# Second feed-forward product of 14 token blocks by Strassen's seven products, the first in pairs

## Chip, cores and metric

The kernel runs on one core of a Trainium2 chip. The metric is the device time of one execution in microseconds (us). TensorE (PE) multiplies, VectorE (DVE), ScalarE (ACT) and GpSimd (POOL) do the elementwise work, SyncE (SP) issues the DMAs.

## What is computed

Three stages on 8 x 576 tokens of 512 features, in fp32:

```python
scores = scale * np.matmul(q_c, k_c.transpose(0, 1, 2, 4, 3))      # attention inside chunks of 64 tokens, 8 heads
...
xn = (x - mu) / np.sqrt(var + 1e-06) * g_ln                        # feed-forward, 512 -> 2048 -> 512
ch = np.maximum(xn @ w_ch1, 0.0) @ w_ch2
return (x + ch).astype(np.float32)
...
h = x @ w_in                                                       # second stage: gated unit, mixing along the 576 tokens
h = 0.5 * h * (1.0 + np.tanh(c * (h + 0.044715 * h ** 3)))
v_s = np.einsum('ts,bsd->btd', w_sg, v_n) + b_sg[None, :, None]
return (x + gated @ w_out).astype(np.float32)
```

## The kernel before

The 4608 tokens are 36 tiles of 128, and two tiles make one of NB = 18 blocks of 256 tokens. Every fp32 product is made of three fp16 matmuls: each operand is split into a high and a low part, and high x high, high x low and low x high are added in PSUM.

**Attention** of a tile: QK (L273), maximum and difference (L308, L309), exp, sum (L314), reciprocal (L302), transposes (L283) through `pt`, PV (L292), and DVE's L322, which scales the result into the tile's x. All three PE steps of a tile use one PSUM pair (`pair1`), so the next tile's QK waits for L322. LayerNorm follows (L352, L353, L355), and `hl`, the split of it (ACT L358, POOL L360), goes by a transposing DMA into `xT`.

**Feed-forward** of a block b: `ff1(b, f)` for f = 0 to 15 multiplies 128 of the 2048 hidden features (12 matmuls of 256 columns into one bank, L511); ACT makes the high part (L515), DVE the low part (L516). `ff2(b, f)` uses them as stationary operand against 128 rows of w2 (6 matmuls of 512 columns, L532) and adds into two banks, one for each tile, over all 16 f. After the last, DVE adds the banks to x (two L544), SP stores x (L547, `x2d`), DVE takes its maximum (L184).

The order on each engine is made by a planner: each step is recorded with `op` (engine, assumed ns, reads, writes, priority), and `Plan.run` places them by these assumed times. In the FF blocks ff2 runs two f behind ff1, and the attention of later blocks is interleaved on PE. The first blocks go another way: the first products of blocks 0 and 1 are kept (`late`) until w2 is ready, and ff2 of blocks 1, 0 and 3 runs in rows of sixteen units without ff1 between.

While blocks 4 and on run, the **weights of the second stage** are prepared (`prep`: loads, L380 on DVE, L581 on ACT, a maximum through PE with `par`, a split with POOL L610), and the first x2 tiles are read back (`open_x2`, `first_x2`). After the last block the **second stage** follows: its first units are `v_unit` (L830); in it DVE's L818 and L916 and POOL's L856 and L906 are elementwise operations with two inputs in SBUF.

Of the kernel before, what the change touches and what calls it, by code (L numbers as in the profile page):

```python
# [127 lines left out]
def fused_kernel(ctx: ExitStack, tc, qkv, w1, w2, g1, w_in, w_out, wsgt, wsgs, g2, b_sg, out):  # L128
# [31 lines left out]
    mxc = small.tile([P, 5], F32, name="mxc")  # L160
# [76 lines left out]
    def palloc(tag, bufs, shape, dt, pool=None):  # L237
        return plan.buf(tag, bufs, lambda: (pool or pa).tile(shape, dt, tag=tag, name=tag, bufs=bufs))
# [215 lines left out]
    def scale_w2():  # L454
# [109 lines left out]
    def prep(nm, srcs):  # L564

        pr = 9000
        n = len(srcs)
# [500 lines left out]
```

## Time and profile before

| | |
|---|---|
| median of 3 runs | 1296.22 us (1293.89 to 1296.97) |
| profiled execution | 1294.67 us, span 1292.6 us |
| busy | PE 1246.9, DVE 672.2, ACT 477.2, POOL 260.2 us |
| mean granted clock of TensorE | 0.995 |

Attention of the first tiles and the preparation of w1 and w2 take the first part of the span, the FF blocks last until 877 us, the second stage takes the rest. "Idle before" or a bracket behind a row is the time in which the engine stood still ahead of that instruction, and behind the arrow what ended it. A matmul is listed with its latency; matmuls overlap, so the step from one start to the next is shorter. A clock of 1.00 is full speed.

### The profile page before, as it was taken

The page shows a single profiled execution, that of the slowest core. Times are in us where ns is not written, and L with a number is a line of the kernel's source. Part 1 is how long each engine was busy: PE and PEld are TensorE (multiplying, and loading weights), DVE is VectorE, ACT ScalarE, POOL GpSimd, SP SyncE. Part 2 cuts the span into 40 slices and gives each one's busy share as a digit, 9 for nine tenths or more (in the row PEclk, how much of TensorE's full clock was granted, in tenths as well). Part 3 has the DMA queues.
Part 4 walks back from the last instruction along what each step waited for, and adds up shares of the span by engine and source line. Part 5 has one row for each costly group of instructions (what it writes and reads, how often), then busy time and mean ns, then how long its engine had stood idle before and what let it go on. Part 6 is the DMA issues. An engine that isn't in the chain of part 4 may idle for free.

```text
span 1292.6 us, 23846 instructions
## 1 busy us (share of the span) xinstructions
PE 1246.9 (96%) x10111; PEld 774.2 (60%) x10111; DVE 672.2 (52%) x1381; ACT 477.2 (37%) x911; POOL 260.2 (20%) x291
## 2 busy tenths in 40 slices
PE   6899999999999999999999999999999998999998
PEld 4677645676666666666666666654544543554453
DVE  7895126434443244334324433217879479469564
ACT  5776302465321121122122112105745636537330
POOL 3342201042010010001001001003425035134120
PEclk9999999999999999999999999999999999999999
DMA  9963006522721131123113110002031240330101
GB/s 308 248 227 84 1 33 186 203 83 87 143 74 50 42 83 50 50 66 71 54 42 83 48 28 17 17 17 90 17 58 50 98 72 10 139 58 17 74 1 74
DMA packets 106378, 101.87 MB, mean 79 GB/s; under 512 B 79648, under 2 KB 79648, under 8 KB 106272
## 3 DMA queue, kind: packets, MB, share of 16 engines
q1 hardware_dynamic: 106272, 100.36, 27.9%
q8 instruction: 79, 1.29, 0.4%
q14 instruction: 27, 0.22, 0.1%
HBM read 62.59 MB, written 18.87 MB: 63 GB/s over the span
## 4 chain that ended last, share of the span: by engine, by line
PE 77%; DVE 12%; ACT 4%; DMA 3%; POOL 1%; issue 1%; SPq 1%; DVEq 0%; ACTq 0%; POOLq 0%
PE bank L511 25%; PE pair L532 23%; PE pb L892 8%; PE pb L874 7%; PE pb L954 4%; PE bank L532 3%; PE pb L830 2%; DVE gv L818 2%; DMA straw<-in_w 2%; DVE bs L838 1%; PE pair L273 1%; DVE gl L229 1%; DVE q L811 1%; PE pair L292 1%; ACT top L375 1%
## 5 line engine op out<-in xcount | busy, mean ns | idle before, releaser
L511 PE MATMUL bank<-xT,w1h 128*128 128x256 f16 x2304 | 393.0, 274 | 8.1 <-DVE hTl L516 3.7
L511 PE MATMUL bank<-xT,w1l 128*128 128x256 f16 x1152 | 315.1, 273 | 0.0
L516 DVE SCALAR_TENSOR_TENSOR hTl<-bank,hTh 128x256 f16<-128x256 f32 x256 | 108.0, 423 | 341.5 <-ACT hTh L515 340.1
L532 PE MATMUL pair<-w,hTh 128*128 128x512 f16 x896 | 266.5, 379 | 0.0
L511 PEld LDWEIGHTS <-w1h 128*128 128x128 f16 x2304 | 221.1, 98 | 70.7 <-issue 10.1
L515 ACT ACTIVATE hTh<-bank 128x256 f16<-128x256 f32 x256 | 97.7, 383 | 417.1 <-PE bank L511 416.9
L532 PE MATMUL pair<-w,hTl 128*128 128x512 f16 x448 | 169.8, 379 | 0.0
L532 PEld LDWEIGHTS <-hTh 128*128 128x128 f16 x1024 | 99.7, 98 | 75.1 <-issue 0.2
L511 PEld LDWEIGHTS <-w1l 128*128 128x128 f16 x1152 | 113.1, 98 | 13.5
L347 POOL TENSOR_SCALAR rs<-mv 128x1 f32<-128x1 f32 x36 | 8.6, 239 | 505.4 <-DVE mv L353 504.9
L830 PE MATMUL pb<-win,x2T 128*128 128x512 f16 x432 | 95.3, 379 | 0.9 <-DVE x L544 0.9
L874 PE MATMUL pb<-x2T,win 128*128 128x384 f16 x576 | 94.6, 326 | 0.0
L954 PE MATMUL pb<-wout,gh 128*128 128x512 f16 x288 | 85.7, 379 | 7.6 <-DVE x L959 7.6
L892 PE MATMUL pb<-wsg,vh 128*128 128x512 f16 x288 | 88.0, 380 | 0.0
L532 PEld LDWEIGHTS <-hTl 128*128 128x128 f16 x512 | 50.1, 98 | 60.4
L808 ACT ACTIVATE h<-pb,e2g 128x384 f32<-128x384 f32 (+1 forms) x84 | 52.0, 619 | 91.7 <-PE pb L874 57.9
L906 POOL TENSOR_TENSOR uT<-uT,vs 128x512 f32<-128x512 f32 x32 | 48.6, 1518 | 177.7 <-DVE vs L902 177.7
L874 PEld LDWEIGHTS <-win 128*128 128x128 f16 x576 | 56.2, 98 | 37.5
L811 DVE SCALAR_TENSOR_TENSOR q<-q,h 128x384 f32<-128x384 f32 (+1 forms) x84 | 52.0, 619 | 43.1 <-ACT q L809 43.1
L830 PEld LDWEIGHTS <-x2T 128*128 128x128 f16 x432 | 41.3, 98 | 50.4 <-issue 2.0
L360 POOL TENSOR_TENSOR hl<-xn,hl 128x512 f16<-128x512 f32 x36 | 44.5, 1237 | 70.2 <-ACT hl L358 70.0
L892 PE MATMUL pb<-wsg,vl 128*128 128x512 f16 x160 | 56.5, 380 | 0.0
(181 smaller groups left out, 1675.8 us busy)
## 6 DMA issues: line engine op xcount, KB each, us to landing
qk<-in_qkv SPq DMA_DIRECT2D x36, 512.0 KB, 3.9
straw<-in_w SPq DMA_DIRECT2D x16, 1023.8 KB, 6.4
v<-in_qkv SPq DMA_DIRECT2D x36, 256.0 KB, 3.2
x2d<-x SPq DMA_DIRECT2D x36, 256.0 KB, 2.0
x<-x2d SPq DMA_DIRECT2D x36, 256.0 KB, 4.7
out<-x SPq DMA_DIRECT2D x36, 256.0 KB, 2.0
raw<-in_w_in SPq DMA_DIRECT2D x4, 1023.8 KB, 5.0
raw<-in_w_out SPq DMA_DIRECT2D x2, 1023.8 KB, 4.8
```

The lines of the kernel that those rows point to most:

```text
L360: o(lo[0], lo[1], lambda: lo[2].tensor_tensor(out=hl.t[:, 1], in0=xn.t, in1=hl.t[:, 0], op=ALU.subtract), rd=[xn], wr=[hl])
L511: nc.tensor.matmul(acc, lhsT=w[j][:, k, fc], rhs=xT.t[:, x, k], start=(n == 0), stop=(n == 11))
L515: op("ACT", 260, lambda: nc.scalar.activation(out=h[0].t, in_=acc, func=AF.Relu), rd=[kb], wr=[h[0]], prio=-100)
L516: op("DVE", 340, lambda: nc.vector.scalar_tensor_tensor(out=h[1].t, in0=acc, scalar=0.0, in1=h[0].t, op0=ALU.max, op1=ALU.subtract), rd=[k ...
L532: nc.tensor.matmul(acc[i], lhsT=h[x].t[:, c], rhs=w2t[j][:, f % 2, y], start=(f == 0 and n == 0), stop=(f == NF - 1 and n == 2),)
L808: nc.scalar.activation(out=h, in_=ps, func=AF.Copy, scale=e2g[:, g:g + 1])
L811: nc.vector.scalar_tensor_tensor(out=q, in0=q, scalar=1.0, in1=h, op0=ALU.add, op1=ALU.mult)
L830: nc.tensor.matmul(ps, lhsT=x[:, k, c], rhs=w[:, k, 512:1024], start=(n == 0), stop=(n == 11))
L874: nc.tensor.matmul(ps, lhsT=w[:, k, fc], rhs=x[:, k, c], start=(n == 0), stop=(n == 11))
L892: nc.tensor.matmul(ps, lhsT=v[:, fc], rhs=w[:, 0:512], **f)
L906: nc.gpsimd.tensor_tensor(out=uv, in0=uv, in1=vs, op=ALU.mult)
L954: nc.tensor.matmul(ps, lhsT=x[:, k, c], rhs=w[:, k], start=(n == 0), stop=(n == 11))
```

## The change

Four things change for blocks 4 to 17 (B0 = 4), and three around them.

`ff1p(b, j)` makes two units of ff1, f = 2j and 2j + 1, into the two halves of one bank (24 matmuls of 256 columns, L631 after). Four blocks of 128 x 128 come of it: two feature halves by two token halves. ACT takes the relu of all (L645), DVE makes four sums and differences (L652), ACT the high part of the seven operands (128 x 896, L655), and the low part comes from DVE for even j and from POOL for odd j (L657).

`ff2p(b, j)` multiplies by Strassen's scheme (Winograd's form): seven products P1 to P7 of 128 x 256 x 128, three matmuls of 256 columns each (L677), in the order 1, 6, 5, 7, 2, 3, 4, in place of eight. It runs two pairs behind ff1p. P1 and P6 add into one bank of `pair0`, P5 and P7 into the other, P2 and P3 into bank 6, P4 into bank 7. At j = 7 ten DVE operations L698 add them to the x of the two tiles, in place of two L544.

`sums_w2(j)` makes the right operands from w2, once for all blocks, while ff2 of block 3 runs: for each of eight j ACT L581, DVE L584 (1024 wide), four DVE L594 (256 wide), ACT L599 and L600, POOL L603 (768 wide) and L604 (256 wide).

Around them: `prep` of the second stage's weights is cut in two, and its second half (`halve`) is recorded behind blocks 5, 6 and 7; `open_x2` and `first_x2` come behind all FF blocks; the SBUF pools of attention are closed and opened again for the new operands, and the FF intermediates lie in one fixed tile (`arena`, two buffers of each kind).

```diff
+    def sums_w2(j):
...
+        op("ACT", 950, lambda: nc.scalar.activation(
+            out=flat(), in_=w[:, :, 0], func=AF.Copy, scale=0.25
+        ), rd=["sums", k], wr=[bf], prio=pr)
+        op("DVE", 1140, lambda: nc.vector.scalar_tensor_tensor(
+            out=flat(), in0=w[:, :, 1], scalar=0.25, in1=flat(), op0=ALU.mult, op1=ALU.add
+        ), rd=[k], wr=[bf], prio=pr)
...
+            for o, x, y in (
+                (t[:, 0], b[:, 0, 1], b[:, 0, 0]), (t[:, 1], b[:, 1, 1], t[:, 0]),
+                (t[:, 2], b[:, 1, 1], b[:, 0, 1]), (t[:, 3], t[:, 1], b[:, 1, 0]),
+            ):
+                nc.vector.tensor_tensor(out=o, in0=x, in1=y, op=ALU.subtract)
...
+            nc.gpsimd.tensor_tensor(out=w2s[j][:, 1], in0=tf.t[:, 1:4], in1=w2s[j][:, 0], op=ALU.subtract)
...
+    def ff1p(b, j):
...
+            op("PE", 1310, mm, rd=[xT], wr=[kb], prio=1000 + nff[0])
...
+            op("ACT", 580, lambda: nc.scalar.activation(
+                out=o.t[:, 0:4].rearrange("p n t -> p (n t)"), in_=acc, func=AF.Relu, scale=0.5
+            ), rd=[kb] + ar, wr=[o], prio=-100)
...
+                for z, x, y, f in ((4, 0, 2, ALU.add), (5, 4, 1, ALU.subtract), (6, 1, 0, ALU.subtract), (7, 3, 5, ALU.subtract)):
+                    nc.vector.tensor_tensor(out=a[:, z], in0=a[:, x], in1=a[:, y], op=f)
...
+            lo = ("POOL", 2000, nc.gpsimd) if j % 2 else ("DVE", 1000, nc.vector)
+            op(lo[0], lo[1], lambda: lo[2].tensor_tensor(
+                out=h.t[:, 1], in0=o.t[:, 1:8], in1=h.t[:, 0], op=ALU.subtract
+            ), rd=[o], wr=[h], prio=-100)
...
+    def ff2p(b, j):
...
+        for p in (1, 6, 5, 7, 2, 3, 4):
+            op("PE", 326, lambda p=p: mm(p), rd=[h, f"w2_{j}"], wr=[f"P{p}"] + extra, prio=1000 + nff[0])
+        if j == 7:
...
+            for p, c, x, d in (
+                (1, "a", x0, 2), (1, "a", x1, 2), (6, "b", x0, 1), (6, "b", x1, 2), (5, "b", x0, 1), (5, "b", x1, 1),
+                (7, "b", x1, 2), (2, "a", x0, 0), (3, "a", x0, 1), (4, "n", x1, 0),
+            ):
...
-        for b in range(5, NB + 1):
-            for f in range(NF + 2):
-                if f >= 2:
-                    ff2(b - 1, f - 2)
-                if b < NB and f < NF:
-                    ff1(b, f)
-            block(b + 2)
-            if b == NB - 3:
-                op(None, 0, open_x2, rd=["stC"], wr=["x2L"], prio=0)
-                first_x2()
+        for b in range(B0, NB):
+            for j in range(8):
+                rest = ff1p(b, j)
+                todo.append((b, j))
+                if len(todo) > 2:
+                    ff2p(*todo.pop(0))
+                rest()
+            block(b + 2)
+            if b in (B0 + 1, B0 + 2, B0 + 3):
+                half[b - B0 - 1]()
...
+        op(None, 0, open_x2, rd=["stC"], wr=["x2L"] + ATT, prio=0)
+        first_x2()
```

By the added lines the names move: attention's QK L273 is L289 after, the transposes L283 are L299, PV L292 is L308, L308 is L324, L309 L325, L314 L330, L302 L318, L322 L338, L352 L369, L355 L372, the eviction L544 is L563 where it is kept, the maximum L184 is L197, v_unit's L830 is L1013.

The order on PE at the end of a block, before (`pair_63` is the two banks of the block's sums, `w_7` the last rows of w2):

```order
L532 LDWEIGHTS hTh
L532 MATMUL pair_63<-w_7_161,hTh 128x512
L532 LDWEIGHTS hTl
L532 MATMUL pair_63<-w_7_161,hTl 128x512
L511 LDWEIGHTS w1h_138 [waits DMAHW6_49,DMAHW3_49]
L511 MATMUL bank_65<-xT,w1h_138 128x256 [waits DVE_49]
L511 LDWEIGHTS w1h_138
L511 MATMUL bank_65<-xT,w1h_138 128x256
```

The same place after (`w2s` are the sums of w2, `arena` the seven left operands). The first row is the last matmul of P1, the next three products are P6, and the row with a wait is the first of P5:

```order
L677 MATMUL pair_63<-w_7_166,arena 128x256
L677 LDWEIGHTS arena
L677 MATMUL pair_63<-w2s_2496,arena 128x256
L677 LDWEIGHTS arena
L677 MATMUL pair_63<-w2s_2496,arena 128x256
L677 LDWEIGHTS arena
L677 MATMUL pair_63<-w2s_2496,arena 128x256
L677 LDWEIGHTS arena
L677 MATMUL pair_63<-w_7_166,arena 128x256 [waits DVE_49]
L677 LDWEIGHTS arena
L677 MATMUL pair_63<-w_7_166,arena 128x256
```

Before, nothing of the block's last products waits, and ff1 units follow; after, P5 waits for DVE in the middle of the last ff2p. The first matmul of the next block's P1 has the same wait.

The order on DVE at a block's end, before: the two evictions, the maxima, and then L322 of the next attention tile.

```order
L516 SCALAR_TENSOR_TENSOR hTl<-bank_66,hTh 128x256 [waits Activation_49]
L544 SCALAR_TENSOR_TENSOR x<-pair_63,c_c_1738,x 128x512 [waits PE_49]
L544 SCALAR_TENSOR_TENSOR x<-pair_63,c_c_1738,x 128x512
L184 TENSOR_REDUCE x2mx<-x 128x1 [waits DVE_49]
L516 SCALAR_TENSOR_TENSOR hTl<-bank_68,hTh 128x256 [waits Activation_49]
L184 TENSOR_REDUCE x2mx<-x 128x1 [waits DVE_49]
L516 SCALAR_TENSOR_TENSOR hTl<-bank_65,hTh 128x256 [waits Activation_49]
L322 TENSOR_TENSOR x<-pair_64,rd 128x2x4x64 [waits DMAHW0_49,DVE_49]
```

After, with the low part of a pair ahead and the next pair's sums behind. The first row of evictions stands for P1 into both tiles:

```order
L657 TENSOR_TENSOR arena<-arena 128x896 [waits PE_49,Activation_49]
L698 SCALAR_TENSOR_TENSOR x<-pair_63,c_c2a,x 128x512 [waits PE_49] x2
L698 SCALAR_TENSOR_TENSOR x<-pair_63,c_c2b,x 128x256 [waits DVE_49]
L698 SCALAR_TENSOR_TENSOR x<-pair_63,c_c2b,x 128x512 [waits DVE_49]
L698 SCALAR_TENSOR_TENSOR x<-pair_63,c_c2b,x 128x256 [waits DVE_49] x2
L698 SCALAR_TENSOR_TENSOR x<-bank_67,c_c2a,x 128x256 [waits PE_49]
L698 SCALAR_TENSOR_TENSOR x<-pair_63,c_c2b,x 128x512 [waits DVE_49]
L698 SCALAR_TENSOR_TENSOR x<-bank_67,c_c2a,x 128x256
L698 SCALAR_TENSOR_TENSOR x<-bank_68,c_c2n,x 128x256 [waits DVE_49,PE_49]
L652 TENSOR_TENSOR arena<-arena 128x128 [waits Activation_49]
L652 TENSOR_TENSOR arena<-arena 128x128 [waits DVE_49]
```

Two evictions of 512 columns became ten of 512 or 256, of which the first waits for PE behind P6.

The order on DVE where block 5's attention runs, before (`win` is a second-stage weight):

```order
L380 SCALAR_TENSOR_TENSOR win<-raw,top 128x1024 [waits DMAHW2_49,Activation_49]
L516 SCALAR_TENSOR_TENSOR hTl<-bank_66,hTh 128x256 [waits Activation_49]
L322 TENSOR_TENSOR x<-pair_64,rd 128x2x4x64 [waits DMAHW3_49,DVE_49]
L352 BN_STATS bs<-x 128x6 [waits DVE_49]
L516 SCALAR_TENSOR_TENSOR hTl<-bank_68,hTh 128x256 [waits Activation_49]
L353 BN_AGGR mv<-bs 128x2 [waits DVE_49]
L516 SCALAR_TENSOR_TENSOR hTl<-bank_65,hTh 128x256 [waits Activation_49]
L516 SCALAR_TENSOR_TENSOR hTl<-bank_66,hTh 128x256 [waits Activation_49]
```

At the same attention tiles after, in the transition from block 3 to block 4 (`tf` and `bf` are the sums of w2, `arena` the FF operands):

```order
L317 TENSOR_SCALAR sm<-sm 128x8
L318 RECIPROCAL rd<-sm 128x8 [waits DVE_49]
L594 TENSOR_TENSOR tf<-bf 128x256
L594 TENSOR_TENSOR tf<-bf,tf 128x256 [waits DVE_49]
L594 TENSOR_TENSOR tf<-bf 128x256
L594 TENSOR_TENSOR tf<-tf,bf 128x256 [waits DVE_49]
L657 TENSOR_TENSOR arena<-arena 128x896 [waits Activation_49]
L652 TENSOR_TENSOR arena<-arena 128x128 [waits Activation_49]
L652 TENSOR_TENSOR arena<-arena 128x128 [waits DVE_49]
L652 TENSOR_TENSOR arena<-arena 128x128
L652 TENSOR_TENSOR arena<-arena 128x128 [waits DVE_49]
L338 TENSOR_TENSOR x<-pair_64,rd 128x2x4x64 [waits DMAHW2_49,PE_49]
```

L338, for which the next tile's QK waits, stands behind a group of sums of w2, the low part of the first pair and the sums of the second; before it, L322 had one preparation step and one L516 ahead of it.

## Rows read from the trace of the kernel before

**Rows 1.** The page, first part: busy us, share of the span and instructions.

```profile
PE 1246.9 (96%) x10111; PEld 774.2 (60%) x10111; DVE 672.2 (52%) x1381; ACT 477.2 (37%) x911; POOL 260.2 (20%) x291
```

**Rows 2.** Windows: three stretches of one block period, of which the first and third.

```profile
core 0: us, PE busy (x) PEld busy (x) DVE busy (x) ACT busy (x) POOL busy (x), PEclk, DMA share, GB/s
404.16:449.64 45.48, 45.48 (x426) 31.03 (x424) 17.75 (x38) 9.64 (x22) 3.80 (x6) 1.00 0.21 59
...
586.08:631.56 45.48, 45.48 (x425) 31.03 (x424) 17.76 (x38) 9.64 (x22) 3.80 (x6) 1.00 0.25 59
```

**Rows 3.** The chain that ended last, in one block: start, us, what.

```profile
404.16 2.59 PE pair L532 x12
406.75 2.62 PE bank L511 x24
```

**Rows 4.** Waits of PE between 187 and 360 us.

```profile
engine line waited for: us in total, times, longest us
PE pair L273 <- DVE x L322: 3.1, 2, 2.6
PE bank L511 <- DVE hTl L516: 2.1, 1, 2.1
PE bank L189 <- DVE red L184: 0.9, 1, 0.9
```

**Rows 5.** Windows behind the two longest of these stops, columns as in the second group.

```profile
243.20:248.20 5.00, 5.00 (x58) 3.77 (x58) 3.52 (x8) 1.72 (x5) 0.74 (x2) 0.66 0.79 269
332.90:337.90 5.00, 4.93 (x51) 3.39 (x52) 4.28 (x10) 1.69 (x4) 1.36 (x3) 0.66 0.70 120
```

**Rows 6.** Timeline at a block's end: start us, us, engine, line, operation.

```profile
451.85 0.38 PE L532 MATMUL pair<-w,hTl 128*128 128x512 f16 x1
...
452.27 1.41 DVE L544 SCALAR_TENSOR_TENSOR x<-pair,c_c,x 128x512 f32<-128x512 f32 x2 [1.75 <-PE pair L532]
```

**Rows 7.** Groups of instructions: busy us, mean ns of one, idle before.

```profile
L516 DVE SCALAR_TENSOR_TENSOR hTl<-bank,hTh 128x256 f16<-128x256 f32 x161 | 68.3, 424 | 240.0 <-ACT hTh L515 239.0
L515 ACT ACTIVATE hTh<-bank 128x256 f16<-128x256 f32 x161 | 61.9, 384 | 321.3 <-PE bank L511 321.3
L360 POOL TENSOR_TENSOR hl<-xn,hl 128x512 f16<-128x512 f32 x18 | 20.8, 1158 | 34.7 <-ACT hl L358 34.7
L544 DVE SCALAR_TENSOR_TENSOR x<-pair,c_c,x 128x512 f32<-128x512 f32 x22 | 15.5, 746 | 19.2 <-PE pair L532 19.2
L322 DVE TENSOR_TENSOR x<-pair,rd 128x512 f32<-128x512 f32 x18 | 12.4, 686 | 10.0 <-PE pair L292 10.0
L358 ACT ACTIVATE hl<-xn 128x512 f16<-128x512 f32 x18 | 11.3, 626 | 9.5 <-DVE xn L355 9.5
L302 DVE RECIPROCAL rd<-sm 128x8 f32<-128x8 f32 x17 | 3.4, 203 | 0.6
...
L485 POOL TENSOR_TENSOR w<-cw,w 128x1024 f16<-128x1024 f32 x8 | 17.1, 2133 | 29.7 <-ACT w L484 29.5
L434 ACT ACTIVATE w1h<-cw 128x1024 f16<-128x1024 f32 x8 | 8.4, 1051 | 1.7 <-POOL cw L429 1.7
L436 DVE TENSOR_TENSOR w1l<-cw,w1h 128x1024 f16<-128x1024 f32 x3 | 3.6, 1215 | 1.0 <-ACT w1h L434 1.0
```

**Rows 8.** L818 and L916 (ns min/median/max), and timelines where POOL runs beside.

```profile
L818 DVE SCALAR_TENSOR_TENSOR uT<-q,h x48: 545/551/1626, 912.5 to 1256.2; 128x384 f32<-128x384 f32 x48
...
L916 DVE TENSOR_TENSOR uT<-uT,vt x8: 825/828/833, 940.4 to 1265.9; 128x256 f32<-128x256 f32 x8
...
912.99 2.88 POOL L856 TENSOR_TENSOR vl<-gv,vh 128x512 f16<-128x512 f32 x2
...
914.77 1.51 DVE L818 SCALAR_TENSOR_TENSOR uT<-q,h 128x384 f32<-128x384 f32 x1
...
929.39 1.70 POOL L906 TENSOR_TENSOR uT<-uT,vs 128x512 f32<-128x512 f32 x1 [11.62 <-DVE vs L902]
...
929.89 1.63 DVE L818 SCALAR_TENSOR_TENSOR uT<-q,h 128x384 f32<-128x384 f32 x1
```

**Rows 9.** Timeline at the end of the FF blocks.

```profile
876.19 0.38 PE L532 MATMUL bank<-w,hTl 128*128 128x512 f16 x1
...
877.42 2.32 PE L830 MATMUL pb<-win,x2T 128*128 128x512 f16 x10 [0.85 <-DVE x L544]
```

More of the change, by code (lines that the diff above doesn't have):

```diff
@@ L38 @@
 NB = NT // 2
+B0 = 4
 GC = math.sqrt(2.0 / math.pi)
@@ L212, in par @@
         nscr[0] += 1
-        k, c = f"scr{nscr[0] % 3}", nscr[0] % 3 * 160
-        scr = bank[6][:, c:c + 160]
+        if pr < 1000:
+            k, c = f"scr{nscr[0] % 3}", nscr[0] % 3 * 160
+            scr = bank[6][:, c:c + 160]
+        else:
+            k, scr = "pair1", pair[1][:, 0, 0:160]
         pr = min(pr, 500)
@@ L551, in fused_kernel, with open_sums @@
     bW = {"top": Buf("topB", None)}
-    def open_b():
+    ATT = [f"{n}{k}" for n in ("qk", "v", "mx", "pm", "sm", "rd", "bs", "mv", "rs", "hl") for k in range(2)] + ["pt", "xn"]
+    w2s = {}
+    def open_sums():
         late.__exit__(None, None, None)
         stL.__exit__(None, None, None)
+        close_pool("att")
+        open_pool("w2s", bufs=1, side="right")
+        open_pool("att", bufs=2, side="right")
+        for j in range(8):
+            w2s[j] = pools["w2s"][1].tile([P, 2, 3, 256], F16, name=f"w2s{j}")
+        open_pool("sums", bufs=2)
@@ L556, in open_b @@
+    def open_b():
+        close_pool("sums")
         wB = ctx.enter_context(tc.tile_pool(name="wB", bufs=1))
@@ L727, in fused_kernel @@
             ff2(0, f)
+        used = ["cw0", "cw1", "cw2"] + [f"straw{k}" for k in range(2)] + ["x0", "x1", "xT2", "top0", "top1"]
+        used += [f"late{n}{k}" for n in "hl" for k in range(32)]
+        op(None, 0, open_sums, wr=used + ATT + ["sums"], prio=0)
         for f in range(NF):
             ff2(3, f)
-        pools = ["cw0", "cw1", "cw2"] + [f"straw{k}" for k in range(2)] + ["x0", "x1", "xT2", "top0", "top1"]
-        pools += [f"late{n}{k}" for n in "hl" for k in range(32)]
-        op("DVE", 600, open_b, wr=pools + ["stB", "topB"], prio=0)
@@ L733, in fused_kernel @@
-        prep("win", [w_in[k] for k in range(4)])
-        prep("wout", [w_out[k] for k in range(2)])
+        for j in range(8):
+            sums_w2(j)
+        op(None, 0, lambda: None, wr=[f"hT{n}{k}" for n in "hl" for k in range(16)] + ["arena"], prio=0)
+        op("DVE", 600, open_b, wr=["bf0", "bf1", "tf0", "tf1", "stB", "topB"], prio=0)
+        half = [prep("win", [w_in[k] for k in range(4)]), prep("wout", [w_out[k] for k in range(2)])]
         wv = wsgt.rearrange("(k p) e -> k p e", p=P)
-        prep("wsg", [wv[k] for k in range(4)] + [wsgs])
+        half.append(prep("wsg", [wv[k] for k in range(4)] + [wsgs]))
@@ new lines, in fused_kernel @@
+        todo = []
+        for b in range(B0, NB):
+            for j in range(8):
+                rest = ff1p(b, j)
[3 more added lines that the diff above has]
+                rest()
+            block(b + 2)
+            if b in (B0 + 1, B0 + 2, B0 + 3):
+                half[b - B0 - 1]()
+            if b == B0 + 3:
+                op(None, 0, close_st, rd=["wsg_s"] + done, wr=["Braw", "Btmp", "topB", "stC"], prio=0)
+        for b, j in todo:
+            ff2p(b, j)
```

134 lines of the change are left out of this document (115 added, 19 removed).

## Prediction

> **What bounds the kernel now.** I read the page first: PE is busy 1246.9 of the span's 1292.6 us [rows 1]. In the feed-forward blocks it is the bound without a gap: three windows one block period long (45.48 us) show PE busy for all of it at clock 1.00, while DVE has 17.75, ACT 9.64 and POOL 3.80 us [rows 2]. The chain of waits there is PE after PE: two ff1 units (24 matmuls 256 wide) take 2.62 us, two ff2 units (12 matmuls 512 wide) 2.59 [rows 3]. So work taken from PE there is worth its full time, as long as nobody else becomes late. [...]
>
> **The change, part by part.**
>
> *Fewer matmuls.* A 256-wide matmul costs 2.62/24 = 0.109 us, a 512-wide one 2.59/12 = 0.216 [rows 3]. ff2 of a block was 16 x 6 x 0.216 = 20.7 us; now it is 8 pairs x 7 products x 3 x 0.109 = 18.3. That is 2.37 per block, 33.2 in 14 blocks. (Exactly an eighth would be 2.6; the narrow matmul is a little dearer per column.) ff1 keeps its count.
>
> *The stalls of before.* The window of 187 to 360 us holds the preparation of the second stage's weights (L380, L581, L610) and the first x2 tiles beside FF blocks. Both are moved: the first to blocks 4 to 8, the second behind all FF blocks. I take the 9.5 us off and book what comes in their place below.
>
> *Block end.* In before the two evictions L544 (1.41 us) lie under the next ff1 units: the next ff2 begins 2.6 us later [rows 6]. Now P1 and P6 share a bank and the order shows that P5's first matmul waits for the first of ten DVE evictions L698, which waits for P6. With T the start of the block's last ff2p: P6's last matmul starts 5 x 0.109 = 0.54 later and takes 0.27 (T+0.82); the eviction begins about 0.04 later, as L544 does behind L532 in [rows 6], and takes 0.75 like L544 [rows 7]; PE goes on 0.05 later, at T+1.65 in place of T+0.65. So 1.0 us per block. The other evictions (four 512 wide at 0.75, six 256 wide at 0.42 like L516, ten hand-overs of 0.05) end at T+6.9; the eighth, for which the next block's P1 waits, at about T+5.95, when PE comes to it at 1.65 + 5 x 0.33 + 2.62 = T+5.9. Another 0.1. So 1.1 x 14 = 15.4. Bounds: 0 (the wait isn't there) and 2.1 per block (next but one paragraph).
>
> *Load of the other engines in a block.* DVE gives up 16 L516 (6.8) and gets eight groups of four 128-wide sums (no row has one; between 0.20 for 8 elements and 0.42 for 256 I take 0.30, so 1.2 a group), four lo of 896 (between 0.69 for 512 and 1.22 for 1024: 1.06) and 4 us more evictions: 17.75 - 6.8 + 9.6 + 4.2 + 4.0 = 29. POOL gets four lo of 896 (between 1.16 and 2.13: 1.9): 3.8 + 7.6 = 11.4. ACT, with 0.6 and 0.94 in place of two 0.38, comes to 16 [rows 7]. All far below 44, and ff2p runs two pairs behind ff1p, 9.8 us of PE work, of which relu, sums, hi and lo need about 5. What isn't covered is the first attention QK after a block end: it waits for L338, which stands on DVE behind the ten evictions, two groups of sums and two maxima: T + 6.9 + 2.4 + 1.3 + 0.7 = T+11.3, and PE comes to it at 5.95 + 2.29 + 36 x 0.109 = T+12.2. Slack 0.9, booked at nothing; if one POOL lo (1.9) gets in the way it costs 1.0.
>
> *The transition, blocks 3 to 4.* The sums of w2 are new work for DVE, ACT and POOL while PE runs ff2(3). PE has, from the end of ff2(0) to the third QK behind it, 96 matmuls of ff2(3) (20.7), two attention tiles (3.8, what a block's 45.48 leaves over its 20.9 of ff1 and 20.7 of ff2), 72 matmuls of ff1p (7.9) and three of ff2p: 32.7 us. DVE has before the L338 for which that QK waits: 2.7 (last evictions and maxima of ff2(0)), seven L584 at 1.22 (as L436), seven groups of L594 at 1.55 (four 256 wide, 0.42 as L516, with some overlap) [rows 7], two groups of sums and a lo (3.5), two attention tiles without the last LayerNorm steps (2 x 4.1 - 1.4 = 6.8, from the block's 17.75), and the evictions and maxima of block 3 (2.7): 35.1. By these sums alone PE waits 2.4 us, with hand-overs some 5. But POOL's and DVE's operations with two SBUF inputs exclude each other in the trace: L818 takes 0.55, but 1.51 where it starts while POOL's L856 runs, and it ends 0.4 us after that does (916.28 after 915.87); beside L906 it is 1.63, and again 0.4 us is left after POOL's end. L916, 256 wide and in L906's stretch, takes 0.83 [rows 8]. POOL has 7 x (1.65 + 0.67) for L603 and L604 (between and below its 1.16 and 2.13) and one hl: 17.4. DVE's two-input work is 8.5 + 10.9 + 3.5 = 22.9. One after the other they are 40.3; of DVE's other 9.5 us about half falls beside POOL: 40.3 + 4.8 + 2.7 - 32.7 = 15, and 1 for the last sums behind it. I take 16, since exclusion is what the rows show; bounds 2 and 21 (none of the other work beside POOL).
> [...]
>
> *Preparation of the second weights* in blocks 4 to 8: eleven chunks, each with a POOL operation of up to 2.13 and several on DVE and ACT. I book 3.0, what it cost in its old place (2.14 + 0.86); bounds 0 and 10 (0.9 for each POOL operation).
>
> *Handover to the second stage.* In before L830 starts 0.85 us after PE's last matmul, released by L544 [rows 9]. Now it waits for the tenth eviction, T+6.9, with PE done at T+3.45: 3.45, so 2.6 more. The last pair's lo on POOL has no ff1p left as cover: its hi shares a buffer with pair 5, so 0.94 + 1.9 = 2.84 stand against the 2.29 of the one ff2p between: 0.7 late with hand-overs. And the stops of 2.14 and 2.60 lost 1.7 of clock each; this one is longer. Together 5.0.
>
> Sum: 1292.6 - 33.2 - 9.5 + 15.4 + 16 + 3 + 5 = 1289.3 span; the profiled execution took 1294.67, 2.07 over its span: **1291**. It is itself 1.55 below the median of the runs (1296.22); against that the forecast is 0.4% less. About 0.3% (3.9 us) is what a measurement of this kernel can tell from no change.
>
> **Rivals.**
> B, transition cheap: POOL and DVE share without loss, or the sums run further ahead. For it: L584 and L594 alone are 19 us of DVE under 33 of PE. Against: [rows 8]. 1291 - 11 = 1280.
> C, slower: the exclusion reaches every block. Where a lo on POOL (1.9 us) starts before the last of the sums behind the evictions, L338 comes 1.5 later, and the QK waits. Place: the first QK after each block end; it decides once the delay exceeds the 0.9 of slack; at 1.0 to 1.2 per block it is 14 to 17 us: 1306. For it: by the sums the POOL lo would start at T+9.2, when DVE is at the fourth of its sums, so it is a matter of 0.1 us. Against: whoever is first goes, and DVE should be.
> D, the change does nothing for PE: 256-wide products with changing weights don't run at 0.109. Against: ff1 has just that shape at 0.109. 1324.
> E, block ends free (P5 doesn't wait): 1276.
> F, preparation at its upper bound: 1298.
>
> **Numbers.** Forecast 0.42 (own range 1284 to 1299; 0.22 of it is faster by over 0.3%, 0.20 within), B 0.20, C 0.24 (0.02 of it within), D 0.03, E 0.08, F 0.03. Faster: 0.22 + 0.20 + 0.08 = 0.50; within: 0.20 + 0.02 + 0.03 = 0.25; slower: 0.22 + 0.03 = 0.25. The range 1275 to 1307 leaves out half of E, a third of C, D: under 0.2.
>
> **What would show it.** Block period 44.2 with one idle of 1.0 before P5 (L677 after DVE L698); 43.1 would be E, over 45 C. PE idle of about 16 in all between the end of ff2(0) and the middle of block 4, at QK (after L338) and before L677 (after L657), with L594 longer than 0.45 beside L603; if L594 is 0.4 throughout, B. 3.4 idle before the first L1013. No PE idle from the x2 loads in blocks 5 to 8. Wrong it is most of all if the transition costs under 8 or the first QK of each block waits over 0.5.

## The result, and the profile after

The changed kernel takes 1302.47 us (median of 7 runs, 1299.27 to 1305.36) against 1296.22 of the kernel before on the same chip: ratio 1.0054 (95% interval 1.0032 to 1.0077), slower by half a per cent. The profiled execution took 1301.82 us, its span is 1300.0, the mean granted clock 0.986.

The page of the changed kernel, first part, against [rows 1]:

```profile
PE 1229.3 (95%) x11119; PEld 876.2 (67%) x11119; DVE 875.0 (67%) x1816; ACT 575.4 (44%) x935; POOL 393.6 (30%) x363
```

PE is busy for 17.6 us less, yet the span is 7.4 longer: PE stands still for 70.7 us in place of 45.7. DVE has 203 us more work, POOL 133. Windows of the changed kernel show where (columns as in [rows 2]): `ff2` of block 3 alone, the period of block 4, those of blocks 5, 6 and 7, and one of the steady periods behind them:

```profile
213.12:245.12 32.00, 26.83 (x202) 12.69 (x201) 28.85 (x44) 14.01 (x20) 15.66 (x12) 0.89 0.34 108
245.12:303.75 58.63, 52.19 (x629) 44.37 (x628) 50.73 (x93) 33.62 (x49) 26.42 (x20) 0.94 0.61 180
303.75:353.20 49.45, 45.71 (x500) 38.86 (x500) 35.39 (x78) 31.66 (x46) 20.82 (x14) 0.97 0.27 85
353.20:399.79 46.59, 45.76 (x500) 39.05 (x500) 33.42 (x74) 19.56 (x26) 15.65 (x12) 0.96 0.21 58
399.79:446.62 46.83, 44.47 (x500) 38.14 (x500) 34.41 (x74) 21.95 (x32) 18.04 (x15) 1.00 0.21 57
491.00:535.38 44.38, 43.42 (x496) 37.99 (x496) 28.78 (x67) 15.56 (x22) 11.32 (x10) 1.00 0.22 61
```

The steady period fell from 45.48 [rows 2] to 44.38 us, with PE 0.96 short of busy. In the first two windows DVE is busy for 90% and 87%, PE idle for 5.2 and 6.4 us, and the mean clock is 0.89 and 0.94; the periods of blocks 5 to 7 are 2 to 5 us longer than the steady one.

The waits of PE over the whole span name the new ones; the first sum is the block ends, the third the end of the last block:

```profile
PE pair L677 <- DVE x L698: 16.0, 14, 2.6
PE pair L289 <- DVE x L338: 7.6, 5, 3.2
...
PE pb L1013 <- DVE x L698: 3.5, 1, 3.5
```

The timeline at two block ends: the start of the next block's first pair, then, a block later, the wait of P5 for P1's tile (in brackets the idle time and what ended it):

```profile
539.93 0.74 DVE L698 SCALAR_TENSOR_TENSOR x<-pair,c_c2b,x 128x512 f32<-128x512 f32 x1
...
540.33 0.27 PE L631 MATMUL bank<-xT,w1l 128*128 128x256 f16 x1
...
540.72 0.49 PE L677 MATMUL pair<-w,arena 128*128 128x256 f16 x3
...
579.23 0.49 PE L677 MATMUL pair<-w2s,arena 128*128 128x256 f16 x3
579.76 0.75 DVE L698 SCALAR_TENSOR_TENSOR x<-pair,c_c2a,x 128x512 f32<-128x512 f32 x1 [1.26 <-PE pair L677]
580.57 0.49 PE L677 MATMUL pair<-w,arena 128*128 128x256 f16 x3 [0.84 <-DVE x L698]
```

P5 (580.57) starts 1.34 us behind P6's first matmul (579.23) where 0.33 would be the step: 1.01 lost. The next block's P1 starts 0.39 behind the last matmul of `ff1p`, where the step is 0.11: 0.28 more, since the last eviction that reads its tile ends at 539.93 + 0.74 = 540.67. No QK waits in a steady period.

Of the 14 waits of P5, eleven are of 0.84. Those at the ends of blocks 4, 5 and 7 are of 2.61, 2.33 and 1.80: there the first eviction stands on DVE behind a late low part, as at the end of block 5, where L657 takes 1.94 beside a POOL operation of the preparation (1.09 is its median on DVE):

```profile
350.21 2.13 POOL L785 TENSOR_TENSOR win<-tmp,win 128x1024 f16<-128x1024 f32 x1 [0.84 <-ACT win L782]
...
351.34 1.94 DVE L657 TENSOR_TENSOR arena<-arena 128x896 f16<-128x896 f32 x1 [1.10 <-ACT arena L655]
...
353.99 0.49 PE L677 MATMUL pair<-w,arena 128*128 128x256 f16 x3 [2.33 <-DVE x L698]
```

Four of PE's stops in the transition, from its timeline:

```profile
231.51 0.69 PE L308 MATMUL pair<-v,pt 64*64 64x64 f32 x32 [1.73 <-ACT pt L332]
...
236.86 1.14 PE L289 MATMUL pair<-qk 64*64 64x64 f32 x32 [3.25 <-DVE x L338]
...
254.46 0.28 PE L677 MATMUL pair<-w,arena 128*128 128x256 f16 x1 [0.53 <-DVE arena L657]
257.78 1.13 PE L289 MATMUL pair<-qk 64*64 64x64 f32 x32 [3.04 <-DVE x L338]
```

With one of 0.90 at 273.60 they are 9.45 us. Around the two of over 3 us the mean granted clock was 0.50 to 0.68 for 8 us each; in windows of half a us it was 0.50 from 236.0 to 242.5 and from 256.5 to 263.0. By PE's busy time in the windows of 4 us an estimated 3.14 x 0.50 + 4.00 x 0.32 + 2.22 x 0.47 + 4.00 x 0.38 = 5.4 us more are lost:

```profile
236.00:240.00 4.00, 3.14 (x37) 1.69 (x38) 3.97 (x8) 1.70 (x3) 2.49 (x2) 0.50 0.20 43
240.00:244.00 4.00, 4.00 (x14) 1.50 (x12) 4.00 (x6) 1.82 (x4) 3.50 (x3) 0.68 0.24 94
256.00:260.00 4.00, 2.22 (x38) 1.80 (x39) 4.00 (x7) 1.44 (x2) 2.53 (x3) 0.53 0.03 5
260.00:264.00 4.00, 4.00 (x25) 3.00 (x24) 3.93 (x11) 1.27 (x2) 1.34 (x3) 0.62 0.99 363
```

And while PE waits, DVE's sums are slow where a POOL operation runs (timeline, two places; 0.42 is the median of L594, 1.22 that of L584):

```profile
226.39 1.64 POOL L603 TENSOR_TENSOR w2s<-tf,w2s 128x768 f16<-128x768 f32 x1
226.46 1.85 DVE L594 TENSOR_TENSOR tf<-bf 128x256 f32<-128x256 f32 x1 [0.56 <-POOL w L604]
...
240.42 1.64 POOL L603 TENSOR_TENSOR w2s<-tf,w2s 128x768 f16<-128x768 f32 x1 [1.91 <-ACT w2s L599]
...
240.67 2.47 DVE L584 SCALAR_TENSOR_TENSOR bf<-w,bf 128x1024 f32<-128x1024 f16 x1
```

L594 ends 0.28 us after L603 does, so it did at most 0.14 of its 0.42 us of work beside it, much as L818 in [rows 8].

### The profile page after: what moved, and what is told of

It is laid out like the page before. It is cut to its first block, busy times and chain, and to the rows that moved or that the text cites. A ratio compares the mean times of both kernels' runs of the same rounds, so it can differ in the third digit from the quotient of the medians.

```text
span 1300.0 us, 26627 instructions
## 1 busy us (share of the span) xinstructions
PE 1229.3 (95%) x11119; PEld 876.2 (67%) x11119; DVE 875.0 (67%) x1816; ACT 575.4 (44%) x935; POOL 393.6 (30%) x363
## 4 chain that ended last, share of the span: by engine, by line
PE 52%; DVE 13%; ACT 1%; issue 0%; POOL 0%; DVEq 0%; ACTq 0%; POOLq 0%
PE bank L631 14%; PE pair L677 8%; PE pb L1075 7%; PE pb L1057 7%; PE bank L677 5%; PE pb L1137 4%; DVE x L698 4%; PE pb L1013 2%; DVE gv L1001 2%; DVE bs L1021 1%; DVE gl L245 1%; DVE q L994 1%; PE pb L1076 1%; PE pair L308 1%; PE pair L289 1%; DVE gv L1031 1%
## 5 line engine op out<-in xcount | busy, mean ns | idle before, releaser
L631 PE MATMUL bank<-xT,w1h 128*128 128x256 f16 x1792 | 302.6, 274 | 0.0
L677 PEld LDWEIGHTS <-arena 128*128 128x128 f16 x2352 | 229.1, 98 | 53.1 <-issue 22.6
L631 PE MATMUL bank<-xT,w1l 128*128 128x256 f16 x896 | 244.8, 273 | 0.0
L652 DVE TENSOR_TENSOR arena<-arena 128x128 f32<-128x128 f32 x448 | 148.9, 375 | 114.6 <-ACT arena L645 110.6
L657 POOL TENSOR_TENSOR arena<-arena 128x896 f16<-128x896 f32 x56 | 106.3, 1897 | 318.2 <-ACT arena L655 301.9
L631 PEld LDWEIGHTS <-w1h 128*128 128x128 f16 x1792 | 173.6, 98 | 22.0
L655 ACT ACTIVATE arena<-arena 128x896 f16<-128x896 f32 x112 | 106.2, 949 | 161.2 <-PE bank L677 106.5
L645 ACT ACTIVATE arena<-bank 128x512 f32<-128x512 f32 x112 | 66.4, 593 | 168.0 <-PE bank L631 166.5
L677 PE MATMUL pair<-w,arena 128*128 128x256 f16 x672 | 111.0, 274 | 17.5 <-DVE x L698 15.2
L677 PE MATMUL pair<-w2s,arena 128*128 128x256 f16 x672 | 111.1, 275 | 0.8 <-DVE x L698 0.8
L1013 PE MATMUL pb<-win,x2T 128*128 128x512 f16 x432 | 97.0, 384 | 3.5 <-DVE x L698 3.5
L631 PEld LDWEIGHTS <-w1l 128*128 128x128 f16 x896 | 87.9, 98 | 10.5
L677 PE MATMUL bank<-w,arena 128*128 128x256 f16 x672 | 93.3, 275 | 0.0
L657 DVE TENSOR_TENSOR arena<-arena 128x896 f16<-128x896 f32 x56 | 65.7, 1174 | 32.9 <-ACT arena L655 32.2
```

The lines of the kernel that those rows point to most:

```text
L631: nc.tensor.matmul(acc[:, y * 256:y * 256 + 256], lhsT=w[j][:, k, fc], rhs=xT.t[:, x, k], start=(n == 0), stop=(n == 11),)
L645: op("ACT", 580, lambda: nc.scalar.activation(out=o.t[:, 0:4].rearrange("p n t -> p (n t)"), in_=acc, func=AF.Relu, scale=0.5), rd=[kb] + ...
L652: nc.vector.tensor_tensor(out=a[:, z], in0=a[:, x], in1=a[:, y], op=f)
L655: op("ACT", 950, lambda: nc.scalar.activation(out=h.t[:, 0], in_=o.t[:, 1:8], func=AF.Copy), rd=[o] + ar, wr=[h], prio=-100)
L657: op(lo[0], lo[1], lambda: lo[2].tensor_tensor(out=h.t[:, 1], in0=o.t[:, 1:8], in1=h.t[:, 0], op=ALU.subtract), rd=[o], wr=[h], prio=-100)
L677: nc.tensor.matmul(acc, lhsT=h.t[:, x, n], rhs=r(y), start=(first and j == 0 and m == 0), stop=(j == 7 and m == 2), skip_group_check=True,)
```

## Experiments

Theory at the start: the three losses are the shared tile at the block end, DVE and POOL shutting each other out in the transition, and the preparation of the second weights, which stands beside blocks that need DVE more than the old ones did. Rival: it is the order on the engines, or simply the amount of work.

In e5, e7 and e8 block 4, in the old form, reads parts of w2 that the sums have overwritten, so its output is of other operands; its operations are as many and as large as in the old form.

**e1: the two sums of the block end in tiles apart.** `pair0` is closed in `open_sums` and opened again as two tiles of one bank each; the evictions' order is fixed by priority.

```diff
+        a, b = (q.tile([P, 512], F32, name=f"acc{n}") for n in "ab")
+        POS.update({1: (a[:, 0:256], True), 6: (a[:, 256:512], False), 5: (b[:, 0:256], True), 7: (b[:, 256:512], False)})
-                op("DVE", 650 if d == 2 else 420, ev, rd=[f"P{p}"], wr=[x], prio=-120)
+                op("DVE", 650 if d == 2 else 420, ev, rd=[f"P{p}"], wr=[x], prio=-140 + n)
```

> The kernel after, with the two banks of the sums P1/P6 and P5/P7 as two separate PSUM tiles in place of one, and the evictions in the order P1, P6, P5, P7, P2, P3, P4 by priority. Theory: P5 waits for an eviction of P1 only because both lie in one tile, and a block end costs 1.0 there and 0.3 at the next block's P1. Then the idle of 0.84 before P5 is gone in all 14 blocks, the block period falls from 44.38 to between 43.1 and 43.6 us, and the time by 11 to 18: 1284 to 1291. Rival: ten evictions are too much for DVE and the same time is waited for at the next block's P1, P5 or P2: period 44.1 or more, time 1298 to 1303.

Measured: 1282.97 us, a little under the theory's range, ratio to before 0.9903 (0.9873 to 0.9933). The timeline at a block's end: P5 follows P6 by 0.33 and doesn't wait for the eviction:

```profile
569.18 0.49 PE L677 MATMUL acca<-w2s,arena 128*128 128x256 f16 x3
569.51 0.49 PE L677 MATMUL accb<-w,arena 128*128 128x256 f16 x3
569.71 1.41 DVE L698 SCALAR_TENSOR_TENSOR x<-acca,c_c2a,x 128x512 f32<-128x512 f32 x2 [1.26 <-PE acca L677]
```

The windows of blocks 5, 6 and 7 and of a steady one:

```profile
304.14:351.71 47.57, 44.38 (x502) 38.16 (x501) 35.31 (x78) 31.38 (x46) 20.81 (x14) 1.00 0.29 88
351.71:395.25 43.54, 42.58 (x488) 36.85 (x487) 33.31 (x73) 19.67 (x26) 15.63 (x12) 1.00 0.22 62
395.25:440.80 45.55, 45.12 (x511) 39.03 (x510) 34.32 (x74) 21.95 (x33) 18.03 (x15) 1.00 0.22 59
526.61:569.71 43.10, 43.10 (x498) 38.01 (x497) 28.68 (x66) 15.55 (x23) 11.31 (x10) 1.00 0.26 63
```

A steady period has no idle time left: 44.38 − 43.10 = 1.28 per block, both waits of the block end, 18 us in 14 blocks, of 19.5 between the medians. P1's and P5's banks were never the same; what P5 waited for was the eviction of the other bank of its tile. (The fixed order and the tiles went in together; which of them took the 0.28 away isn't told apart.)

**e2 and e3: what the sums of w2 cost.** e2 lets POOL write zeros where it wrote the low parts of the sums; e3 leaves the sums out and uses quarters of w2 itself as operands.

```diff
-            nc.gpsimd.tensor_tensor(out=w2s[j][:, 1], in0=tf.t[:, 1:4], in1=w2s[j][:, 0], op=ALU.subtract)
+            nc.gpsimd.memset(w2s[j][:, 1], 0.0)
```
```diff
-        for j in range(8):
-            sums_w2(j)
```

> The kernel after, with POOL writing zeros as the low parts of the sums of w2 (L603, L604), an operation that reads nothing; the low parts of these sums are left out. Theory (exclusion of DVE and POOL operations that read SBUF is what makes the transition long): no L594 or L584 much over its shortest time, the PE stops at QK, PV and the first L677 (1.73, 3.25, 0.53 and 3.04 us between 230 and 258 us) shrink to 3 in all or less, and the two falls of the granted clock there are gone or one is left: 9 to 13 us less. Rival (DVE's own work under ff2 of block 3 is too long, POOL does not matter): stops of over 6 us stay, and less than 4 us is gained.

> The kernel after without the sums of w2: quarters of w2 stand in their place as right operands, so the products are of the wrong operands and of the same size; the pools are opened as before. Theory: all of the transition's loss, 9.5 us of PE stops and 6.8 of clock, comes from the sums: 14 to 18 us less, and no stop over 0.5 us between 215 and 275 us. Rival (a part comes from closing and opening the attention pool, whose loads of q and k begin only then): stops of over 3 us stay at QK, behind a DMA, and 10 us or less are gained.

Measured: 1289.65 and 1288.60, one run each, 12.8 and 13.9 under the changed kernel's median (whose own runs lie 6 apart); e3 was to gain 14 to 18. The source view of L594 (ns min/median/max, first and last start), of after and then of e2:

```profile
L594 DVE TENSOR_TENSOR tf<-bf x16: 372/418/1853, 220.3 to 262.8; 128x256 f32<-128x256 f32 x16
```
```profile
L594 DVE TENSOR_TENSOR tf<-bf x16: 374/417/425, 220.4 to 254.8; 128x256 f32<-128x256 f32 x16
```

Beside POOL's zeros, not one of these DVE operations is long; waits for QK between 205 and 300 us fall from 7.3 to 2.5. To take away POOL's reading gains nearly what leaving out all of the sums gains: so by these two runs most of the loss in the transition comes of POOL's work on the low parts, and little of DVE's own 19 us of sums. (The zeros are also written faster, 0.74 and 0.31 us for a mean of 1.83 and 1.02, so POOL's shorter time is part of e2's gain; how large a part isn't told apart.) On DVE's side it is 1.85 for L594 beside L603, which reads, against at most 0.43 beside the zeros. e3 was to be left with no stop over 0.5; it keeps 7.6 us of stops in that window, each of 1.1 or less.

**e4: the moves alone.** The kernel before, with the preparation in halves behind blocks 5 to 7 and the x2 loads behind all blocks.

```diff
+            if b in (5, 6, 7):
+                half[b - 5]()
-            if b == NB - 3:
-                op(None, 0, open_x2, rd=["stC"], wr=["x2L"], prio=0)
-                first_x2()
```

> The kernel before with the two moves of the change alone: the second half of the preparation of the second stage's weights behind blocks 5, 6 and 7, and the first x2 tiles behind all FF blocks; ff1 and ff2 as before. Theory (the prediction's): the 9.5 us of stops and clock of before are gone and at most 3 come back: 1287 to 1290. Rival: the preparation costs as much in its new place, on a DVE with room, as in its old one: 1294 to 1297, so that moving gave nothing.

Measured: 1291.05, ratio 0.9960 (0.9945 to 0.9976): 4.8 us faster, between the theory's range and the rival's. The stop of 2.60 at the x2 loads is gone; the waits of PE between 187 and 870 us that are left:

```profile
PE bank L512 <- DVE hTl L517: 1.9, 1, 1.9
PE bank L190 <- DVE redc L185: 0.8, 1, 0.8
PE pair L274 <- DVE x L323: 0.5, 1, 0.5
```

Of the 9.5 credited for the moves, they bring 4.8: in its new place the preparation costs 1.9 + 0.8 of stops in the old blocks too. The mean granted clock over its whole span is 0.989 against 0.995 before; where it was lower was not shown.

**e5 to e8: is it the order?** All on e1. e5 starts the new form one block later, so that block 4's old form lies behind the sums; e6 spreads the preparation, two chunks a block from block 5 on, each step behind the stored x of the block before; e7 does both; e8 is e5 with two empty steps on SP that restore the order of the kernel before in blocks 1 to 3.

```diff
-B0 = 4
+B0 = 5
+        block(5)
+        for f in range(NF + 2):
+            if f < NF:
+                ff1(4, f)
+            if f >= 2:
+                ff2(4, f - 2)
```
```diff
-            if b in (B0 + 1, B0 + 2, B0 + 3):
-                half[b - B0 - 1]()
+            if b >= B0 + 1:
+                gate[:] = [f"x2d{2 * b - 2}"]
+                next(steps, None)
```
```diff
+        op("SP", 1460, lambda: None, wr=["qk0"], prio=100, lat=2200)
+        op("SP", 730, lambda: None, wr=["v0"], prio=100, lat=2200)
```

> The kernel with the two PSUM tiles apart, and one block more in the old form: block 4 by ff1 and ff2, Strassen's products from block 5 on, so that the sums of w2 have the 45 us of block 4 over them beside ff2 of block 3. Theory (the transition loses because DVE's and POOL's 40 us of mutually exclusive work stand under 33 us of PE): with 78 us over it hardly a stop is left; the 13 us of stops and 3.4 of clock between 225 and 290 us shrink to 4 or less, one block loses its 2.4: 1269 to 1276. Rival (what stops PE there is the order, sums ahead of attention on DVE, whatever the room): the stops stay above 9 us, 1280 to 1286.

> The kernel with the two PSUM tiles apart, with the preparation of the second stage's weights spread: two chunks a block from block 5 on, each step let go only when the block two before is stored. Theory (blocks 4, 5 and 7 are longer than 43.1 by 4.5 and 2.5 us, and the clock falls there, because preparation and FF work meet on DVE and POOL): the stops of 0.9, 1.2, 0.8, 0.9 and 0.4 us between 300 and 450 us are gone, 4 to 8 us less than with the tiles apart alone: 1275 to 1279. Rival (the same work costs the same wherever it lies, a little in each block): 1281 to 1285.

> Both: Strassen's products from block 5 on, and the preparation spread from block 5 on. Theory: both gains add, as they lie in different stretches: 1264 to 1271. Rival (either of them frees the same engine time): no better than the better of the two by more than 3 us.

> Strassen's products from block 5 on, and two steps in the planner's list that issue nothing but take SyncE's time there as the loads of tile 10's q, k and v did before; with them the order of all engines up to 180 us is that of the kernel before. Theory (the 3.0 us by which the change is late at 189 us come from that order, which the later load of tile 10 re-dealt): 2 to 4 us less than without them. Rival (the 3 us are start-up chance, different in each execution): within 1.5 us.

Measured: 1279.30 (ratio 0.9876, 0.9861 to 0.9891), 1281.15 (0.9894, 0.9877 to 0.9910), 1276.54 (0.9853, 0.9838 to 0.9867) and 1278.56 (0.9871, 0.9856 to 0.9886). e5's stops stay where they were, a QK of 3.2 and transposes of up to 2.9: the sums beside `ff2(3)` make them, whatever form stands behind. e6 is not to be told from e1: its periods are 47.63, 44.07, 43.93, 44.07, 43.85 and 43.93, so a little is lost in many blocks in place of much in a few. e8 is e5 within the intervals, as its rival has it: the order ahead of block 3 costs nothing that shows. None of the four reaches its theory's range, and e7 is 2.8 under e5, as the rival says of it. e6 also prices the preparation a second way: its blocks 5 to 10 are 8.9 us over six periods of 43.10.

**e9 and e10: pacing and room.** e9 paces the sums: three parts j with units 0, 5 and 10 of `ff2(3)`, five with the pairs of block 4. e10 takes e7 and records the sums of part j behind the last use of it by block 4's `ff2`, beside a block in the old form; all of the computation is there, with one block in 14 less in the new form.

```diff
+            if f in (0, 5, 10):
+                sums_w2(f // 5, f"go{f}")
...
+                if b == B0 and j < 5:
+                    sums_w2(j + 3, f"go{b}_{j}")
```
```diff
-        for j in range(8):
-            sums_w2(j)
...
                 ff2(4, f - 2)
+                if f % 2:
+                    sums_w2(f // 2 - 1)
```

> Two PSUM tiles, the preparation spread from block 5 on, Strassen's products from block 4 on, and the sums of w2 paced by PE: three of the eight are let go with units 0, 5 and 10 of ff2 of block 3, the others each with a pair of block 4, three pairs ahead of their use. Theory (the stops of the transition come from the sums standing on DVE ahead of the attention that PE waits for, because all eight are ready at once): the stops at PV, QK and transposes between 225 and 275 us (1.65, 3.25, 1.24, 3.04 and 1.69 in the run with the preparation spread) fall under 3 us in all, and one clock fall or none is left there: 1268 to 1274. Rival (it is the amount of work, whatever its pace): stops over 7 us in all stay, moved into block 4, and the time stays at 1277 to 1282.

> The same with Strassen's products from block 5 on: the sums of part j of w2 are made when block 4's old ff2 has used that part for the last time (which mends the earlier runs with block 4 in the old form: there block 4 used parts of w2 that the sums had already overwritten). Theory: hardly any stop is left between 210 and 350 us, but one block has lost its 2.4 us and the stops were mostly gone with pacing already: 1269 to 1275, no better than with block 4 in the new form by more than 2 us. Rival (amount of work): better than that one by 5 or more.

Measured: e9 1284.71 (0.9922, 0.9891 to 0.9952), e10 **1268.80 (0.9796, 0.9765 to 0.9826)**, the best version, 2.0% under the kernel before. Pacing alone only moved the stops (between 205 and 300 us e9 waits 6.4 for transposes L301 and 4.3 for QK), and e9 lies above both ranges. With pacing and room they go; e10 is 15.9 under e9, which is what the rival (amount of work) was to show: e10 is 7.7 under e7, which differs from it by the place of the sums alone. The windows of e10, `ff2(3)` and the stretch with the sums:

```profile
211.10:234.24 23.14, 23.14 (x198) 11.47 (x197) 16.71 (x30) 7.16 (x9) 1.90 (x3) 1.00 0.49 154
234.24:333.03 98.79, 95.96 (x1058) 74.45 (x1057) 71.70 (x143) 45.27 (x77) 38.50 (x35) 1.00 0.34 90
```

`ff2(3)` takes 23.14 us for the 32.00 of the changed kernel, DVE is busy for 73% beside the sums in place of 87 to 90%, and the clock stays at 1.00.

**e11 and e12: what the preparation costs.** e1 without the loads, conversions and splits of the second weights; POOL writes zeros for them, in e11 at the same place, in e12 behind block 11.

```diff
+            op("POOL", 700, lambda k=k: nc.gpsimd.memset(both(k), 0.0), rd=["stB"], wr=[ck[k]], prio=pr)
-            op("POOL", 2100 * m // 1024, lambda k=k, tmp=tmp: nc.gpsimd.tensor_tensor(
-                out=half(k, 1), in0=tv(tmp), in1=half(k, 0), op=ALU.subtract
-            ), rd=[tmp], wr=[ck[k]], prio=pr)
```

> The kernel with the two PSUM tiles apart, without the preparation of the second stage's weights: POOL writes zeros in their place, and the loads, the rebuilding, the maxima and the splits are left out. Theory (the preparation costs 7 us in the new blocks, in place of the 3.0 that the prediction booked): the periods of blocks 5 to 8, 47.57, 43.54, 45.55 and 42.72 with the tiles apart, become 43.1 each, and the time falls by 6 to 10: 1273 to 1277. Rival (these periods are the rest of the transition, attention catching up): they stay over 43.1 by 4 us or more in all, and the time stays at 1280 to 1284.

> As the run without the preparation, but with its stand-in (POOL's zeros and the maxima of DVE that waited for them) behind block 11, so that nothing stands in block 4 to 8 for it; loads, rebuilding, maxima and splits of the second stage's weights are left out. Theory (preparation costs 5 in blocks 5 to 7, as the first of these runs showed, and some more in block 4, where its DVE steps stand beside the last of the transition): block 4 ends no later after block 3 than 58.5 us (59.78 with the preparation), blocks 5 to 7 stay at 43.9, and the time is 1274 to 1278. Rival (block 4 is as long without it, and what blocks 5 to 7 gain is scatter): block 4 at 59.5 or more, 1279 to 1283.

Measured: 1281.21 (0.9908, 0.9872 to 0.9943) and 1282.85 (0.9908, 0.9879 to 0.9937), both as e1 and in the rivals' ranges, but not for the rivals' reason. The stand-in has a price of its own. In e11 a maximum on DVE stood 3.36 us behind the zeros and held up the attention (timeline):

```profile
281.81 0.15 DVE L199 TENSOR_REDUCE redc<-mxc 128x1 f32<-128x2 f32 x1 [3.36 <-POOL mxc L750]
...
284.00 1.11 PE L301 MATMUL pair<-ident,pm 128*128 128x128 f32 x4 [4.85 <-ACT pm L330]
```

In e12 the stages can be read apart; windows of block 4, of the first of blocks 5 to 8, and of the block where the zeros are written:

```profile
243.69:298.65 54.96, 52.76 (x631) 44.85 (x630) 41.42 (x87) 24.68 (x37) 23.74 (x20) 0.94 0.30 78
298.65:341.75 43.10, 43.10 (x498) 38.00 (x497) 28.73 (x67) 15.55 (x23) 11.29 (x10) 1.00 0.22 63
...
557.24:612.93 55.69, 47.55 (x510) 39.24 (x509) 39.57 (x90) 15.43 (x22) 27.09 (x24) 0.97 0.18 48
```

Without the preparation block 4 takes 54.96 against e1's 59.78, and blocks 5 to 8 take 43.10 each against 47.57, 43.54, 45.55 and 42.72: it costs 4.8 + 7.0 = 11.8 us there. The zeros cost 55.69 − 43.10 = 12.6 later, which is why the total stands still; DVE operations held up behind them (last section) are part of that price.

## Why the prediction was wrong

The sign does not agree: 1291 was foretold, 0.4% faster, and it became slower by 0.5%. The time lies in the range of 1275 to 1307, but outside the forecast's own 1284 to 1299. It lies nearest to rival C's 1306, whose mechanism isn't there. Span against span the sum missed by 1300.0 − 1289.3 = 10.7 us.

- *Fewer matmuls*, −33.2: right. Two `ff2` units took 2.59, a pair takes 2.295; 8 x 0.295 x 14 = 33.0.
- *Block end*, +15.4: the mechanism was right, the size a little low. 1.01 for P5 as foretold (1.0), but 0.28 rather than 0.1 for the next P1, since an eviction of 256 takes 0.476 in place of 0.42: 1.29 x 14 = 18.1, off by 2.7. The period is 44.38 (44.2 foretold). Not foreseen is that a late DVE makes the wait longer, by 1.77, 1.49 and 0.96 behind blocks 4, 5 and 7; this is counted below, with transition and preparation. What wasn't seen is that it need not be there: e1.
- *Load of the other engines*: right in its sizes (steady DVE 28.8 for 29, ACT 15.6 for 16, POOL 11.3 for 11.4; sums at 0.285 each for 0.30, lo 1.09 on DVE and 1.89 on POOL for 1.06 and 1.9), and right that the first QK of a block doesn't wait: rival C isn't there.
- *The transition*, +16: that DVE's sums are held up beside POOL was right (L594 up to 1.85 beside L603, at most 0.43 beside e2's zeros), the size somewhat high. Between the end of `ff2(1)` and the first `v_unit` the span grew from 690.54 to 693.47 us, by 2.93. With −33.0 for products, +18.1 for block ends and +3.15 for the end of the stage (2.67 more idle and 0.48 for the last lo), 2.93 + 33.0 − 18.1 − 3.15 = 14.7 are left for transition, preparation and the stalls of before together; 16 + 3 − 9.5 = 9.5 were booked (the 9.5 taken off are 6.1 of stops [rows 4] and, by a clock of 0.66 in two windows of 5 us [rows 5], an estimated 2 x 5 x 0.34 = 3.4). With 11.8 for the preparation the transition's share is 14.7 + 9.5 − 11.8 = 12.4, near the 12.8 and 13.9 of e2 and e3.
- *Preparation of the second weights*, +3: **this is the step that failed**: "I book 3.0, what it cost in its old place". In its old place it lay beside blocks in which DVE was busy for 17.8 and POOL for 3.8 of 45.5 us [rows 2]; in the new ones it meets 28.8 and 11.3 of 44.4 and costs 11.8 (e1 against e12), above the upper bound of 10 (rival F, given a chance of 0.03). That was read where the block ends are free; in the changed kernel blocks 5 to 7 are 5.07, 2.21 and 2.45 over the steady period, 9.7 in all (blocks 5 to 8 are 7.0 over theirs in e1), and e3, without the sums, keeps 5.4 of that. So the two terms overlap, and the split between them is good to some 3 us. By e3's price for the sums the preparation still costs 14.7 + 9.5 − 13.9 = 10.3. e4 shows the same work among old blocks at 2.7 us of stops. An earlier price was carried into blocks whose slack the change itself had used up, though the same text had worked out the new loads. Part of the miss is hidden in the total, since the transition was booked 3.6 too high.
- *Handover*, +5: right. 3.52 idle (3.45 foretold), 0.48 for the lo (0.7), and an estimated 5 x 0.34 = 1.7 of clock behind it, as a timeline and a window show:

```profile
876.55 0.28 PE L677 MATMUL pair<-w,arena 128*128 128x256 f16 x1 [0.48 <-POOL arena L657]
...
883.32 1.02 PE L1013 MATMUL pb<-win,x2T 128*128 128x512 f16 x4 [3.52 <-DVE x L698]
```
```profile
883.30:888.30 5.00, 4.98 (x16) 1.94 (x16) 1.16 (x2) 0.57 (x1) 0.00 (x0) 0.66 0.89 286
```

The rest, 3.0 us, lies ahead of the change: `ff2(1)` ended at 186.88 us in the profile of before and at 189.85 after. The twelve experiments, all with the same work up to there, end it between 187.4 and 191.6. e4, where the order on every engine up to there is that of before, ends it at 190.13, and e8, which restores that order up to block 3, at 190.52. So 3.0 is within what one execution differs from another; how far the medians share it stays open. Transition and preparation 5.2, block ends 2.7, start 3.0, products 0.2 and the end of the FF blocks −0.4 make the 10.7.

Rivals B (cheap transition) and D (narrow matmuls) are refuted by the profile; E (free block ends) is what e1 makes of the kernel. Open is how much of the preparation's 11.8 is DVE operations made longer beside POOL's (as L657's 1.94 for 1.09) and how much the order on their queues: no run separates them, and spreading it (e6) gained nothing that shows.

## What to carry to other kernels

Saved matmul time is kept only while the engines that pay for it have room (here 33.0 us were saved and the span grew by 7.4); reckon the price of everything else that shares those stretches anew, with the new loads, and don't carry a measured stall across a change that uses up the slack. Two sums that are read out at different times belong in two PSUM tiles, even where they lie in two banks already (e1, which also fixes the order of the evictions: 1.28 us a block). Set one-time preparation beside the stage that leaves DVE and POOL idle, even if a block of the cheaper form has to be given up for it: here the new place of the sums brought 7.7 us (e7 to e10), and giving up the block, worth 2.4 of matmul time, had already paid for itself (e7 is 4.6 under e6).

## What was not expected of the hardware

- Beside POOL's zeros one DVE operation was as short as ever and another was not. L594, a TENSOR_TENSOR with two inputs in SBUF, took at most 0.43 us beside them (e2), and 1.85 beside L603, which reads. But L374, a TENSOR_SCALAR with one tensor as input, took 4.02 beside zeros in e12, where its median is 0.54; it began 0.09 after them and ended 0.28 after the last of them. The zeros differ too (128x2048 in 1.80 us here, 128x768 in 0.74 in e2); what makes the difference was not shown:

```profile
575.93 1.80 POOL L749 MEMSET wout<- 128x2048 f16 x1
576.02 4.02 DVE L374 TENSOR_SCALAR xn<-x,mv,rs 128x512 f32<-128x512 f32 x1 [1.18 <-POOL rs L369]
...
577.71 2.05 POOL L749 MEMSET wsg<- 128x1152 f16 x2
```

- Fourteen executions with the same first 190 us of work reach its end between 186.9 and 191.6 us: a spread of 4.7, more than the 3.0 booked for the preparation. Two of them, before and e4, with the same order on every engine, lie 3.3 apart.
- Around a stop of 3 us the granted clock was 0.50 and 0.68 in two windows of 4, and the estimated 5.4 that the clock lost at two such stops is nearly their own 6.3; after each of the shorter stops of [rows 5] it was 0.66 for 5 us, an estimated 1.7 lost, and in the 10 us behind the stop of 1.80 at the end of block 7 it was 1.00.
